# The lengths that a planner counts for two kinds of matmul, 512 and 288 columns, when it writes out the order of the work

## The chip, the cores and the metric

The kernel runs on one core of a Trainium2 chip. The metric is the device time of one execution in microseconds (us). Engines are named as in the profile: PE is TensorE, PEld its weight loads, DVE is VectorE, ACT is ScalarE, POOL is GpSimd, and SP is SyncE, which here only issues DMAs.

## The reference

The input x has 2048 rows of 576. It is normalised per row, and two things are made of the result: a self-attention with 32 heads of 18 columns, and a bilinear gated feed-forward block of width 4608. Everything is float32.

```python
xn = _layernorm(x)
q, k, v = split(xn @ wqkv)                       # 32 heads, 18 columns each
s = softmax(q @ k.T * 18 ** -0.5) @ v            # per head, 2048 x 2048 scores
s = merged_heads(s) @ wo
g = silu(((xn @ w_gate) * (xn @ w_up)) @ w_down)
out = x + s * g
```

## The kernel before

A first stage normalises x, turns it to columns and makes q, k and v, split into a high and a low part so that products of float32r operands come close to float32. A last stage multiplies the attention's result by `wo` (L1229) and puts the output together. Between them lies the main stage, some nine tenths of the time, and the change concerns it alone.

In the main stage nearly all matmuls have 64 rows of contraction, so two of them run beside each other, one in the upper half of the array (rows 0 to 63) and one in the lower (64 to 127). Each half works through a list of its own:

- *gate and up* products (`gu_op`, L678): 27 matmuls of 512 columns into one PSUM bank. The upper half makes "up" tiles, the lower "gate" tiles. The work is cut into 72 units of 256 hidden columns by 512 rows of x (18 units for each of four chunks of rows), with two tiles in a unit.
- *down* products (`down_op`, L720): 48 matmuls of 288 columns for each unit in each half, in four groups of 12, each group into a bank that DVE then adds to `acc` (`down_end`, L748). Six of the 12 read `hs`, the hidden rows of the half itself; the next six read `hx`, a copy of the other half's rows that DMAs bring (`turn_round`, L710). The last unit's copy is called `hxl`, and its weights `wdl`.
- *scores for the maxima* (`a_item`, L596): one matmul of 512 columns, then a maximum on DVE (L598). There are 2048 of them, one a head, row tile and column block.
- *scores for the exponentials* (`b_item`, L628): the same in the other orientation, then an exponential on ACT (L630), also 2048.

Between stretches of such work stand *visits* (`pv_group`, L639): up to seven row tiles of the exponentials are multiplied by v over the whole height of the array, 28 matmuls at a time, and DVE or ACT adds the result to `oc`. After a head's last visit `finish` (L651 to L656) turns and divides it on DVE and DMAs store it (L659).

The order of all this is written out when the program is built. `order()` keeps a planned clock for each half (`clk`), planned times at which engines and banks come free (`free`, `banks`), and planned landings of DMAs (`moved`). In a loop it takes the half whose clock is behind and gives it either a score, if the goal clock (`a_goal`, `b_goal`) says that one is due and its bank is free, or the next matmul of its list, which `stream()` yields. Each step moves that half's clock on by its length: LONG for a matmul of 512 columns (`a_next`, `b_next` and the gate and up products), SHORT for one of 288. All other durations are absolute numbers: 0.60 us for a maximum on DVE, 0.495 us for an exponential on ACT, 0.859 us for four matmuls of a visit, 0.24 MB per us for a DMA. `span`, and with it `pace`, the distance at which scores are due, is worked out from LONG and SHORT as well. The clock has no part in the execution: there the engines follow their queues and semaphores. Both halves are fed from the one PE queue, in its order.

Of the kernel before, what the change touches and what calls it, by code (L numbers as in the profile page):

```python
# [40 lines left out]
def kernel(  # L41
# [536 lines left out]
    with ExitStack() as mid:  # L578
# [264 lines left out]
            xi[t] = fin["ep"].tile([128, D], FT, name="xi", bufs=8)  # L843
            nc.sync.dma_start(xi[t], x2[rows, :])

        LONG, SHORT = 0.2335, 0.1335

        def stream(r):

# [449 lines left out]
```

## Time and profile before

| | |
|---|---|
| median of 3 runs | 2575.25 us (2573.8 to 2578.24) |
| the profiled execution's own time | 2576.35 us |
| its span on the core | 2574.6 us |
| PE busy | 2558.4 us, 99% of the span |
| DVE, ACT, POOL busy | 74%, 57%, 23% |
| main stage on PE | from 194.78 to 2510.43 us |
| granted TensorE clock | full speed in all slices |

Times within the run count from the start of the span. A matmul's own duration in the trace (389 ns for 512 columns) is longer than the distance at which matmuls of one half follow each other, since they are pipelined, and the two halves overlap. What a matmul costs is therefore read from the starts of matmuls of one half that follow each other without a wait.

### The profile page before, as it was taken

What the parts mean: (1) busy time and instruction counts of PE and PEld (TensorE: products, weight loads), DVE (VectorE), ACT (ScalarE), POOL (GpSimd) and SP (SyncE); (2) the same over time, 40 slices, a digit from 0 to 9 for tenths busy, and PEclk for the clock granted to TensorE, in tenths of its full rate; (3) what the DMA queues carried; (4) which work ended last, traced back from release to release, by engine and by line L of the source; (5) the groups of instructions that cost most, each with busy time, mean ns of one, the idle gap of its engine ahead of it and who ended that gap; (6) DMA issues with size and microseconds to landing.
All of it is one profiled execution on the core that took longest, in us unless ns stands there. A gap on an engine that the chain in (4) does not pass through costs nothing.

```text
span 2574.6 us, 59106 instructions
## 1 busy us (share of the span) xinstructions
PE 2558.4 (99%) x24360; PEld 2080.9 (81%) x24360; DVE 1917.3 (74%) x3377; ACT 1458.4 (57%) x2688; POOL 594.3 (23%) x663
## 2 busy tenths in 40 slices
PE   8999999999999999999999999999999999999999
PEld 7899887778878778877877788877787888887779
DVE  6209777778778888877788888877788888777527
ACT  5222666666655555655555565655555665555561
POOL 3214434434421111111111112111111211111125
PEclk9999999999999999999999999999999999999999
DMA  7799988887785666665686656656686666665567
GB/s 245 234 281 275 273 228 232 225 222 218 220 202 180 179 181 178 171 183 153 179 196 177 172 161 191 178 157 177 169 198 156 177 187 174 174 178 166 155 182 254
DMA packets 195897, 504.57 MB, mean 196 GB/s; under 512 B 58112, under 2 KB 116352, under 8 KB 156588
## 3 DMA queue, kind: packets, MB, share of 16 engines
q1 hardware_dynamic: 185676, 489.05, 67.9%
q0 software_dynamic: 9952, 11.74, 1.7%
q8 instruction: 192, 3.15, 0.6%
q14 instruction: 77, 0.63, 0.1%
HBM read 312.21 MB, written 107.61 MB: 163 GB/s over the span
## 4 chain that ended last, share of the span: by engine, by line
PE 98%; DVE 1%; DMA 1%; ACT 0%; issue 0%; SPq 0%
PE pg L678 35%; PE pg L639 17%; PE pg L720 16%; PE pa L596 11%; PE pb L628 9%; PE pg L402 2%; PE pa L348 2%; PE pb L348 2%; PE pg L1229 1%; PE pa L1229 1%; PE pb L1229 1%; DMA xc<-sx 0%; DMA xin<-in_A_x_dram 0%; PE pg L334 0%; DVE mx L598 0%; DVE xcx L338 0%
## 5 line engine op out<-in xcount | busy, mean ns | idle before, releaser
L598 DVE TENSOR_REDUCE mx<-pa 128x1 f32<-128x512 f32 x2048 | 1361.8, 685 | 150.2 <-PE pa L596 67.4
L630 ACT ACTIVATE pt<-pb 128x512 f32<-128x512 f32 x2048 | 1155.0, 598 | 549.0 <-PE pb L628 464.7
L678 PE MATMUL pg<-xc,wgu 64*128 64x512 f32 x7776 | 1381.0, 389 | 1.5 <-DMA xc<-sx 1.5
L678 PEld LDWEIGHTS pg<-xc,wgu 64*128 64x128 f32 x7776 | 1032.3, 184 | 54.7 <-DMA xc<-sx 3.1
L628 PE MATMUL pb<-pair,ring 64*128 64x512 f32 x2006 | 783.8, 397 | 0.5 <-ACT us L683 0.5
L596 PE MATMUL pa<-pair,ring 64*128 64x512 f32 x2001 | 781.1, 396 | 0.4 <-DVE mx L598 0.4
L720 PE MATMUL pg<-wd,hs 64*128 64x288 f32 x3408 | 531.3, 292 | 1.2 <-DVE acc L748 1.2
L720 PE MATMUL pg<-wd,hx 64*128 64x288 f32 x3408 | 524.6, 292 | 0.0
L720 PEld LDWEIGHTS pg<-wd,hs 64*128 64x128 f32 x3408 | 468.3, 185 | 6.6 <-DVE acc L748 1.9
L720 PEld LDWEIGHTS pg<-wd,hx 64*128 64x128 f32 x3408 | 462.7, 185 | 3.6 <-DMA hx<-hs 0.5
L639 PE MATMUL pg<-pt,vt 128*32 128x512 f32 x4096 | 454.8, 594 | 0.0
L694 POOL TENSOR_TENSOR hs<-us,hs 128x512 fp32r<-128x512 f32 x144 | 186.1, 1292 | 1120.3 <-ACT hs L693 1101.8
L596 PEld LDWEIGHTS pa<-pair,ring 64*128 64x128 f32 x2001 | 362.6, 184 | 92.0 <-issue 47.8
L628 PEld LDWEIGHTS pb<-pair,ring 64*128 64x128 f32 x2006 | 364.0, 184 | 11.3 <-ACT pt L630 1.4
L639 PEld LDWEIGHTS pg<-pt,vt 128*32 128x32 f32 x4096 | 125.5, 110 | 283.8 <-issue 280.7
L645 DVE TENSOR_TENSOR oc<-oc,pg 128x512 f32<-128x512 f32 x69 | 47.5, 688 | 319.2 <-PE pg L639 319.0
L748 DVE TENSOR_TENSOR acc<-acc,pg 128x288 f32<-128x288 f32 x544 | 234.6, 445 | 26.7 <-PE pg L720 24.0
L693 ACT ACTIVATE hs<-us 128x512 fp32r<-128x512 f32 x144 | 91.0, 632 | 155.8 <-DVE us L690 151.7
L659 POOL DMA_DIRECT2D sot<-oc x124 | 64.0, 523 | 327.7 <-DVE oc L656 325.4
L618 POOL DMA_DIRECT2D pair<-mt x128 | 78.0, 615 | 225.2 <-DVE mt L613 218.6
L643 ACT ACTIVATE oc<-pg 128x512 f32<-128x512 f32 x32 | 19.2, 599 | 189.3 <-PE pg L639 189.3
L194 POOL TENSOR_TENSOR wgu<-wraw,wgu 128x384 fp32r<-128x384 f32 x108 | 108.4, 1017 | 68.2 <-ACT wgu L193 47.8
(141 smaller groups left out, 1381.9 us busy)
## 6 DMA issues: line engine op xcount, KB each, us to landing
wgu<-swg SPq DMA_DIRECT2D x102, 1152.0 KB
hx<-hs SPq DMA_DIRECT2D x142, 512.0 KB
wd<-swd SPq DMA_DIRECT2D x50, 1152.0 KB
swg<-wgu SPq DMA_DIRECT2D x36, 1152.0 KB
pair<-sqk SPq DMA_DIRECT2D x192, 144.0 KB
ring<-sqk SPq DMA_DIRECT2D x384, 72.0 KB
swd<-wd SPq DMA_DIRECT2D x18, 1152.0 KB
sqk<-hl SPq DMA_DIRECT2D x32, 512.0 KB
```

The source lines that it names most:

```text
L194: nc.gpsimd.tensor_tensor(w[:, 9 + b:12 + b, :], raw[:, b:b + 3, :], w[:, b:b + 3, :].bitcast(FT), op=OP.subtract)
L348: nc.tensor.matmul(p, wq[b, a], xcs[c][:, e, :], start=n == 0, stop=n == len(PAIRS) - 1)
L596: nc.tensor.matmul(p, q[rows, t * 128:(t + 1) * 128], k[rows, c * 512:(c + 1) * 512], start=True, stop=True)
L598: nc.vector.tensor_reduce(mx[h][:, t, c:c + 1], p, axis=AX.X, op=OP.max)
L628: nc.tensor.matmul(p, k[rows, t * 128:(t + 1) * 128], q[rows, c * 512:(c + 1) * 512], start=True, stop=True)
L630: nc.scalar.activation(pt[t, c], p, AF.Exp, scale=scale)
L639: nc.tensor.matmul(p[32 * c:32 * c + 32, :], vt[h // 2][:, t, 6 * (h % 2):6 * (h % 2) + 32], pt[t, c], start=t == ts[0], stop=t == ts[-1])
L678: nc.tensor.matmul(ps, gw[n][half[r], a, :], xg[i][half[r], e, :], start=k == 0, stop=k == len(TERMS) - 1)
L693: nc.scalar.activation(hj[:, 0, :], h32, AF.Copy)
L694: nc.gpsimd.tensor_tensor(hj[:, 1, :], h32, hj[:, 0, :].bitcast(FT), op=OP.subtract)
L720: nc.tensor.matmul(ps[:, 0:HALF], (hx if k else hs)[u][half[r], j, a, s * 128:(s + 1) * 128], dw[u][half[r], k, j, e, :], start=n == 0, st ...
L748: nc.vector.tensor_tensor(a, a, ps[:, 0:HALF], op=OP.add)
```

## The change

One line gives the planner other lengths for its two kinds of matmul. No instruction is added or taken away: both programs have the same 7776, 6912, 2048, 2048 and 2048 matmuls at L678, L720, L596, L628 and L639, and 74 visits of the same sizes. What changes is the order in which they stand, nearly everywhere in the main stage.

```diff
-        LONG, SHORT = 0.2335, 0.1335
+        LONG, SHORT = 0.2285, 0.1325
```

PE's queue from the last visit on. `wd` is the down weights of the last unit but one, `wdl` those of the last unit. Before:

```order
L628 MATMUL pb<-pair_1153,ring 128x512
L639 MATMUL pg<-pt,vt 32x512 x16
L720 MATMUL pg<-wdl,hs 128x288 x12
L720 MATMUL pg<-wdl,hxl 128x288 x12
L720 MATMUL pg<-wdl,hs 128x288 x12
L720 MATMUL pg<-wdl,hxl 128x288 x12
L720 MATMUL pg<-wdl,hs 128x288 x11
```

Now, with 51 rows of the `wd` products of both halves left out behind the last one shown:

```order
L678 MATMUL pg<-xc,wgu 128x512 x9
L639 MATMUL pg<-pt,vt 32x512 x16
L678 MATMUL pg<-xc,wgu 128x512 x2
L720 MATMUL pg<-wd,hs 128x288
L678 MATMUL pg<-xc,wgu 128x512
L720 MATMUL pg<-wd,hs 128x288
L678 MATMUL pg<-xc,wgu 128x512
L720 MATMUL pg<-wd,hs 128x288 x2
L678 MATMUL pg<-xc,wgu 128x512
L720 MATMUL pg<-wd,hs 128x288 x2
```

Before, only the last unit's down products (48 in each half) stand behind the last visit. Now there are the down products of two units (96 in each half), and ahead of them the last matmuls of the last gate tile: one of the upper half, six of the lower.

The end of these down products, now, where one unit passes to the next:

```order
L720 MATMUL pg<-wd,hs 128x288
L720 MATMUL pg<-wd,hx 128x288
L720 MATMUL pg<-wd,hs 128x288 x4
L720 MATMUL pg<-wd,hx 128x288 x6
L720 MATMUL pg<-wdl,hs 128x288 x12
L720 MATMUL pg<-wdl,hxl 128x288 x12
L720 MATMUL pg<-wdl,hs 128x288 x12
```

The ten matmuls in two rows of four and six are of the lower half alone, which ends the unit later than the upper one; after them both halves begin the last unit together.

DVE's queue at the same place. Here `oc`, `tp` and `rc` belong to `finish` of the last head, `us` to the gate tile (gate times up, L690), `acc` to the down products. Before:

```order
L645 TENSOR_TENSOR oc<-oc,pg 128x512
L651 STREAM_TRANSPOSE tp<-oc 128x512
L654 RECIPROCAL rc<-tp 128x16
L655 TENSOR_TENSOR tp<-tp,rc 128x16x18
L656 STREAM_TRANSPOSE oc<-tp 128x512
L748 TENSOR_TENSOR acc_11514<-acc_11514,pg 128x288 x4
```

Now:

```order
L645 TENSOR_TENSOR oc<-oc,pg 128x512
L651 STREAM_TRANSPOSE tp<-oc 128x512
L654 RECIPROCAL rc<-tp 128x16
L655 TENSOR_TENSOR tp<-tp,rc 128x16x18
L656 STREAM_TRANSPOSE oc<-tp 128x512
L690 TENSOR_TENSOR us<-pg,us 128x512
L748 TENSOR_TENSOR acc_11500<-acc_11500,pg 128x288 x4
```

The last gate tile's multiplication has moved behind `finish` of the last head; before, it stood ahead of the last visit.

SP's queue at the same place: `hxl` is the other half's rows for the last unit, `wor` the weights of the last stage, `o0` to `o2` attention results for it, `sot` the last head's store. Before:

```order
L710 DMA hxl_37573<-hs_37567 64x1024
L710 DMA hxl_37573<-hs_37567 64x1024
L796 DMA wor_37697<-in_A_wo_dram 128x576
L796 DMA wor_37697<-in_A_wo_dram 128x576
L796 DMA wor_37697<-in_A_wo_dram 128x576
L796 DMA wor_37697<-in_A_wo_dram 128x576
L798 DMA wor_37697<-in_A_wo_dram 64x576
L798 DMA wor_37697<-in_A_wo_dram 64x576
L814 DMA o0_37864<-sot_81 128x512
L814 DMA o1_37865<-sot_81 128x512
L814 DMA o2_37866<-sot_81 128x512
```

Now:

```order
L814 DMA o0_37720<-sot_81 128x512
L814 DMA o1_37721<-sot_81 128x512
L710 DMA hxl_37668<-hs_37662 64x1024
L710 DMA hxl_37668<-hs_37662 64x1024
L796 DMA wor_37784<-in_A_wo_dram 128x576
L796 DMA wor_37784<-in_A_wo_dram 128x576
L796 DMA wor_37784<-in_A_wo_dram 128x576
L796 DMA wor_37784<-in_A_wo_dram 128x576
L798 DMA wor_37784<-in_A_wo_dram 64x576
L798 DMA wor_37784<-in_A_wo_dram 64x576
L814 DMA o2_37722<-sot_81 128x512
```

Two loads of attention results have moved ahead of the last `hxl` pair, the third one has moved behind the six loads of `wor`.

## Rows read from the trace of the kernel before

**Rows 1.** The page: busy time, and the chain that ended last.

```profile
PE 2558.4 (99%) x24360; PEld 2080.9 (81%) x24360; DVE 1917.3 (74%) x3377; ACT 1458.4 (57%) x2688; POOL 594.3 (23%) x663
...
PE 98%; DVE 1%; DMA 1%; ACT 0%; issue 0%; SPq 0%
```

**Rows 2.** Waits: engine, line, releaser: us in total, times, longest.

```profile
PE pg L678 <- DMA xc<-sx: 1.5, 3, 1.0
PE pg L720 <- DVE acc L748: 1.2, 2, 0.8
...
PEld pg L678 <- DMA xc<-sx: 3.1, 4, 1.4
```

**Rows 3.** Timeline: start us, us, engine, line. PE, both halves in 512 columns.

```profile
2480.31 0.39 PE L628 MATMUL pb<-ring,pair 64*128 64x512 f32 x1
2480.31 1.75 PE L678 MATMUL pg<-xc,wgu 64*128 64x512 f32 x13
2481.90 0.40 PE L628 MATMUL pb<-ring,pair 64*128 64x512 f32 x1
```

**Rows 4.** Timeline, PE, from the last visit to the last stage.

```profile
2499.56 3.64 PE L639 MATMUL pg<-pt,vt 128*32 128x512 f32 x32
2503.13 1.06 PE L720 MATMUL pg<-wdl,hs 64*128 64x288 f32 x12
...
2505.64 0.95 PE L720 MATMUL pg<-wdl,hxl 64*128 64x288 f32 x12
2506.70 1.42 PE L720 MATMUL pg<-wdl,hs 64*128 64x288 f32 x12
2507.83 1.08 PE L720 MATMUL pg<-wdl,hxl 64*128 64x288 f32 x12
...
2509.42 1.08 PE L720 MATMUL pg<-wdl,hxl 64*128 64x288 f32 x12
2510.43 1.86 PE L1229 MATMUL pa<-wos,hi 128*128 128x288 f32 x12
```

**Rows 5.** Timeline, PE, the main stage's start.

```profile
194.78 0.49 PE L678 MATMUL pg<-xc,wgu 64*128 64x512 f32 x1
...
195.12 0.39 PE L678 MATMUL pg<-xc,wgu 64*128 64x512 f32 x1
```

**Rows 6.** The chain in order of time: one visit of 28.

```profile
295.60 6.14 PE pg L639 x56
```

**Rows 7.** Timeline, DVE, the same place: `finish`, then sums.

```profile
2503.34 0.69 DVE L645 TENSOR_TENSOR oc<-oc,pg 128x512 f32<-128x512 f32 x1 [3.65 <-PE pg L639]
...
2505.59 0.71 DVE L656 STREAM_TRANSPOSE oc<-tp 128x512 f32<-128x512 f32 x1
2506.23 1.51 DVE L748 TENSOR_TENSOR acc<-acc,pg 128x288 f32<-128x288 f32 x4
```

**Rows 8.** Timeline, DVE, ACT, POOL, SP: last gate tile to `hxl`.

```profile
2490.89 0.69 DVE L690 TENSOR_TENSOR us<-pg,us 128x512 f32<-128x512 f32 x1
...
2491.62 0.63 ACT L693 ACTIVATE hs<-us 128x512 fp32r<-128x512 f32 x1
...
2492.33 1.29 POOL L694 TENSOR_TENSOR hs<-us,hs 128x512 fp32r<-128x512 f32 x1 [9.70 <-ACT hs L693]
...
2493.65 1.10 SPq L710 DMA_DIRECT2D hxl<-hs  x2
2494.85 2.58 SPq L796 DMA_DIRECT2D wor<-in_A_wo_dram  x4
```

**Rows 9.** DMA issues: KB each, median us from issue to landing.

```profile
sot<-oc POOLq DMA_DIRECT2D x124, 36.0 KB, 2.8
...
out_dram<-ys POOLq DMA_DIRECT2D x10, 288.0 KB, 5.6
```

**Rows 10.** Timeline, ACT and POOL: splitting the weights of the last stage.

```profile
2500.16 0.68 ACT L834 ACTIVATE wos<-wor 128x576 fp32r<-128x576 f32 x1
...
2500.91 1.42 POOL L835 TENSOR_TENSOR wos<-wor,wos 128x576 fp32r<-128x576 f32 x1 [7.29 <-ACT wos L834]
```

**Rows 11.** Timeline, PE, at the first change of rows of x.

```profile
749.43 0.50 PE L678 MATMUL pg<-xc,wgu 64*128 64x512 f32 x2 [0.98 <-DMA xc<-sx]
```

**Rows 12.** Timeline, PE, a long list beside a short one: first and last.

```profile
738.62 0.39 PE L678 MATMUL pg<-xc,wgu 64*128 64x512 f32 x1
...
739.99 0.39 PE L678 MATMUL pg<-xc,wgu 64*128 64x512 f32 x1
```

## The prediction

> **What bounds the kernel now.** I read the page first. PE is busy 99% of the span, and 98% of the chain that ended last is PE's [rows 1]. So only PE's queue counts. Next come the waits of PE: the longest sums that name another engine or a DMA are 1.5 and 1.2 us [rows 2]. A reader who stops there would say that nothing is left to win. But a matmul stays "busy" in these views while its half runs late, so I read distances between starts instead. In a stretch where both halves run matmuls of 512 columns, seven of the lengths stand between two score matmuls of one half: 2481.90 - 2480.31 = 1.59 us, or 0.227 each [rows 3]. Where both halves run 288 columns, 24 matmuls, 12 in each half, take 2509.42 - 2507.83 = 1.59 us, or 0.1325 each [rows 4]. These are undisturbed lengths.
>
> With them the main stage can be added up from the order. It lasts from 194.78 to 2510.43, or 2315.7 us [rows 4, 5]. Its 74 visits are 72 of 6.14 [rows 6] and two of 3.64 us [rows 4], together 449.4. In each of the 75 stretches between them I counted each half's matmuls, at 0.227 and 0.1325, and took the longer half: 1808.9 us together. The remainder, 57 us, is what restarts behind visits, last matmuls ahead of them, and waits cost, 0.76 us a stretch. A new order can change only this remainder and the balance of the halves.
>
> **What the change does.** It gives the planner lengths nearer to 0.227 and 0.1325 for the 512 and 288 columns; no duration on the chip depends on them. Every engine's and DMA's planned time stays, so the planner now counts some 2% more matmuls into the same wait. I went through the order for what that moves.
>
> *Visits.* 74 as before, of the same sizes, with the same total of matmuls: 0 us.
>
> *Balance.* The same count over the new order gives 1809.8 us, +0.9. Most of it is in the last stretches: in one the lower half has 3.3 us of work more than the upper, since the upper may not yet begin its down products, and behind the last visit it has 1.1 us more. The bounds are 0 (the other half uses the time for a later stretch, which the order hardly allows) and +1.8, if the longer halves' own distances are those of a disturbed stretch too.
>
> *The scores' spacing.* For each score I took the distance, in these lengths, from the score two before it, which used the same bank. Below 1.4 us lie 672 of the maxima before and 682 now, below 1.3 us 276 and 303 of the exponentials. DVE and ACT are asked about as often, and about as soon, as before: 0 us, with -3 to +3 as bounds, a twentieth of the remainder each way.
>
> *The end, where the sum can be followed.* Let V be the start of the last visit, 2499.56 before. Down products resume at V+3.57 [rows 4], and DVE is in `finish` from V+3.78 to 2505.59+0.71, which is V+6.74 [rows 7]. Before, the down products wait for DVE there: two steps of 12 matmuls take 2506.70-2505.64 = 1.06 and 2507.83-2506.70 = 1.13 us where 0.80 is undisturbed, and the last stage starts 0.2 late in the same way, 0.8 us in all.
>
> Now the last gate tile's six matmuls also stand behind V, and its multiplication (0.69) waits in DVE's queue behind `finish`: V+7.43. The casts on ACT (0.63) and POOL (1.29) follow, with the steps of 0.05 between them [rows 8], and SP issues the `hxl` pair from V+9.45; its second DMA, by half of the pair's 1.10, at V+10.0. The lower half's matmuls: restart at V+3.57, 0.11 for the restart (at the main stage's start the second matmul follows after 0.34 instead of 0.227 us [rows 5]), 6 x 0.227, 48 x 0.1325, so it would begin the last unit at V+11.4. But its second group of 12, due at V+6.6, needs one of four banks. The gate's own comes free at V+7.43 and the first down group's only when DVE has added it behind that, so I count 0.9 us of wait: V+12.3. It reads the rows of `hxl` that land last in its tenth matmul, 9 x 0.1325 later, at V+13.5.
>
> When do they land? No row has the landing of this DMA of 256 KB. The nearest are a store of 36 KB at 2.8 and one of 288 KB at 5.6 us [rows 9]. That makes V+12.8 to V+15.6, a wait of 0 to 2.1. I take the middle, 4.2, because the size is that of the longer row while the queue is SP's and not POOL's: V+14.2, a wait of 0.7. Both waits together are 1.6 where there were 0.8, so +0.8, between 0 and +2.2.
>
> *`wor` behind it.* SP starts these loads at V+10.55 now; before, they were issued ahead of the last visit (2494.85 [rows 8]). The last stage begins at V+12.3+48 x 0.1325+0.7 = V+19.4, and its sixth matmul needs the third low part: landing 4.2, a cast of 0.68 and three of 1.42 on POOL [rows 10], V+19.7, against V+20.0. That hides it by 0.3. At 5.6 for the landing it is 1.1 late. I take 0, with bounds 0 and +1.1.
>
> *Chunk boundaries.* At the first change of rows of x PE waits for them [rows 11]; its weight loads wait 3.1 us for `xc` in the whole run [rows 2], all of it there. The DMAs and their readers stand at the same distances in the new order, 12.6 us at the least, counted in lengths. So this wait stays: 0 us.
>
> **Sum.** +0.9 + 0.8 = +1.7 on the profiled execution's own 2576.35 us: 2578.0. The median of the runs shown is 1.1 lower, 2575.25, and the new one is compared with such runs, so I predict 2577.0. The bounds above add up to -3 and +8.1 around the profiled time.
>
> **Rivals.**
>
> *The truer ratio of lengths pays.* The old ratio takes 0.227 x 0.1335/0.2335 = 0.1298 for a short one where it lasts 0.1325. Where one half is in short and the other in long matmuls, the half with the short ones falls 0.0027 us behind the written order with each. In the order before, 2349 of the 6912 stand so. With the new ratio, 0.0009 remains, and 2349 x 0.0018 = 4.2 us can be saved if all of it had been passed on to the end. Against it: where a long list stands beside a short one, seven long ones in a row start 1.37/6 = 0.228 us apart [rows 12], hardly more than the 0.227 beside long ones, so the lag mostly fits into what the halves may run apart. With this and the same waits otherwise, 2577.0 - 4.2 = 2572.8; with a tenth of the remainder (5.7) gone as well, since the scores stand later against DVE, 2567.
>
> The Trainium skill, "TensorE: Matmul & The Clock Gate", Part 3 on row and column tiling, says that matmuls start and end strictly in program order, and only weight loads are pulled ahead. By that rule a half that lags holds up the other at once, and this rival would be paid in full; the trace's 0.228 beside 0.227 shows little of it here.
>
> *A load that arrives late.* The forecast has x at the later chunk boundaries, and the score operands, hidden as before. If the second boundary, whose loads stand 12.7 us ahead of their readers at the least, behaves as the first one does, at a like distance, 3.1 us are added: 2580.1, and 2583.2 if the third, at 14.1 us, does too. For it: one load of a head's keys has moved from 8.3 to 6.0 us ahead of its first reader, close to the longest landing in [rows 9]. Against it: before, the second boundary had loads 12.2 us ahead, and PE has no longer wait for them than those of the first. It decides from about 3.5 us of new waits on.
>
> *The change does nothing.* The order differs in most rows of PE's queue, so this is out; that it does nothing to the time is the forecast.
>
> **Chances.** The forecast, with rests between -5 and +5 us, 0.60. The truer ratio with fewer waits 0.18, the late load 0.22. A measurement here can tell a difference of about 0.2%, 5.2 us, from none: between 2570.1 and 2580.4 is "the same". The ratio alone (2572.8) would still be the same, and becomes faster with the fewer waits; I give 0.17 to that, 0.61 to the same and 0.22 to slower. The range, 2568 to 2584, reaches from the ratio with most of the fewer waits to both boundaries late. The forecast's own is 2573 to 2581.
>
> **What would show it.** Right: 74 visits and PE at 98% of the chain again; PE from the last visit to the last stage some 8.5 us longer than the 10.9 of before (V+19.4), with the lower half waiting for DVE about V+7 and for `hxl` about V+13.5; the stage ahead of it shorter by some 7 us, so that the last stage starts within 3 us of 2512. Wrong: `hxl` landed ahead of its reader (the landing was over-priced); waits for `xc`, `ring` or `pair` at places other than about 745 us (a late load); a remainder well below 57 us in the same count (the ratio pays).

## The result and the profile after

The changed kernel takes 2584.43 us (median of 7 runs, 2582.93 to 2584.98). The ratio to the kernel before is 1.0030, with a 95% interval from 1.0018 to 1.0042. It is slower by 0.3%, some 8 us; forecast were 2577.0 us and no difference. The profiled execution took 2584.43 us too, with a span of 2582.6 us.

The page of after, against [rows 1]: PE is as busy as before, but DVE and the DMAs now have 3% of the chain that ended last, where they had 2%, and PE's share is 96% instead of 98%.

```profile
PE 2559.4 (99%) x24360; PEld 2089.2 (81%) x24360; DVE 1923.5 (74%) x3377; ACT 1463.7 (57%) x2688; POOL 595.2 (23%) x663
...
PE 96%; DVE 2%; DMA 1%; SPq 0%; issue 0%; ACT 0%; POOL 0%; ACTq 0%
```

The waits of PE after, as in [rows 2] (us in total, times, longest). Three of them were not among the long ones before: the maxima on DVE, the `hx` rows, and, in the last line, one wait of 1.8 us in the last stage.

```profile
PE pg L720 <- DVE acc L748: 2.3, 4, 1.0
PE pa L596 <- DVE mx L598: 2.1, 4, 0.7
PE pg L720 <- DMA hx<-hs: 1.9, 2, 1.7
PE pa L1229 <- ACT hi L822: 1.8, 1, 1.8
```

Before, PE waited for the maxima once:

```profile
PE pa L596 <- DVE mx L598: 0.4, 1, 0.4
```

PE from the last visit on, the rows that answer to [rows 4] (start us, us, engine, line, [idle before <-releaser]):

```profile
2494.50 3.64 PE L639 MATMUL pg<-pt,vt 128*32 128x512 f32 x32
...
2501.88 0.40 PE L720 MATMUL pg<-wd,hs 64*128 64x288 f32 x1 [0.50 <-DVE us L690]
...
2508.34 0.67 PE L720 MATMUL pg<-wdl,hxl 64*128 64x288 f32 x6 [0.24 <-DMA hxl<-hs]
...
2513.72 0.53 PE L1229 MATMUL pa<-wos,hi 128*128 128x288 f32 x2
2516.01 2.22 PE L1229 MATMUL pa<-wos,hi 128*128 128x288 f32 x10 [1.76 <-ACT hi L822]
2518.03 2.69 PE L1229 MATMUL pb<-wos,hi 128*128 128x288 f32 x12
2520.56 3.35 PE L1229 MATMUL pg<-wos,hi 128*128 128x288 f32 x24
```

The last visit starts at V = 2494.50, the last stage at 2513.72. Here are the stage's inputs. First the chain in order of time, from the last gate tile's multiplication to the ten matmuls that waited in the last stage:

```profile
2501.17 0.66 DVE us L690
...
2502.57 1.31 POOL hs L694
...
2503.89 0.47 SPq L710
...
2505.05 0.60 SPq L796
...
2506.74 0.48 SPq L796
...
2509.06 6.24 DMA o<-sot
...
2515.32 0.64 ACT hi L822
...
2516.01 2.22 PE pa L1229 x10
```

SP's queue holds, in this order, the two last `hxl` transfers (L710), six loads of `wor` (L796, L798) and the third block of o. It stands still until POOL has the `hs` rows of the last gate tile; then all nine go out within some 5 us. The third block of o is issued ninth and lands after 6.24 us, and PE's third matmul waits for its cast. ACT's casts of the first and the third `wor` load show when these land, and the last row is the third low part on POOL, as in [rows 10]:

```profile
2509.00 0.69 ACT L834 ACTIVATE wos<-wor 128x576 fp32r<-128x576 f32 x1 [6.51 <-DMA wor<-in_A_wo_dram]
...
2512.98 0.69 ACT L834 ACTIVATE wos<-wor 128x576 fp32r<-128x576 f32 x1 [0.38 <-DMA wor<-in_A_wo_dram]
...
2513.74 1.41 POOL L835 TENSOR_TENSOR wos<-wor,wos 128x576 fp32r<-128x576 f32 x1 [0.15 <-DMA wor<-in_A_wo_dram]
```

The same place in windows (us; busy time of PE, PEld, DVE, ACT, POOL; granted TensorE clock as a share of full speed; share of the DMA engines; GB/s):

```profile
2500.00:2504.00 4.00, 3.50 (x52) 3.26 (x51) 3.12 (x8) 0.63 (x1) 1.30 (x1) 1.00 0.00 0
2504.00:2508.00 4.00, 4.00 (x54) 3.86 (x51) 1.95 (x5) 0.00 (x0) 0.00 (x0) 1.00 0.75 179
2508.00:2512.00 4.00, 3.75 (x55) 3.66 (x56) 1.64 (x4) 1.81 (x4) 1.43 (x1) 1.00 1.03 320
2512.00:2516.00 4.00, 2.25 (x30) 1.86 (x26) 2.99 (x6) 1.96 (x5) 2.84 (x2) 1.00 0.97 292
2516.00:2518.00 2.00, 1.99 (x10) 1.99 (x11) 0.90 (x2) 1.10 (x2) 1.39 (x1) 0.67 0.82 249
2518.00:2520.50 2.50, 2.50 (x13) 2.50 (x13) 0.00 (x0) 0.00 (x0) 1.54 (x2) 0.58 0.90 284
```

The DMA engines move nothing for 4 us, are at 0.75 in the next four, and full (1.03 and 0.97) for the 8 us after them. Behind the wait the granted clock falls to its lower level, 1.2 GHz, for some 3.4 us (full speed less 0.67 and 0.58, over 2.0 and 2.5 us): the ten matmuls from 2516.01 and the next twelve take 2.02 and 2.53 us, from group to group, where before, whose first group starts at 2510.43 [rows 4], has 1.70 for a first and 1.59 for a second twelve:

```profile
2512.13 1.76 PE L1229 MATMUL pb<-wos,hi 128*128 128x288 f32 x12
2513.72 3.35 PE L1229 MATMUL pg<-wos,hi 128*128 128x288 f32 x24
```

This is not peculiar to the one profiled execution. A fall of 3.4 us to half the clock takes 1.7 of 2584, or 0.0007, off an execution's mean granted clock. All seven executions of after have a mean of 0.999, while ten of the eleven of e8 (below), in which the wait is gone, have 1.000. In the kernel before, `wor` was issued 15.6 us ahead of the last stage [rows 4, 8] and the DMAs worked at 0.96 while the last visit began:

```profile
2496.00:2500.00 4.00, 4.00 (x36) 3.16 (x38) 1.36 (x3) 3.53 (x7) 0.00 (x0) 1.00 0.96 299
```

From the first to the last matmul of the last stage after takes 63.2 us, before 59.4; from there to the end 5.6 against 4.7. That is 4.7 of the 8.0 us between the two spans. The main stage, up to the last stage's start, is 4.2 longer (2319.9 against 2315.7), and it starts 0.9 earlier.

### The profile page after: what moved, and what is told of

Same layout as the page of the kernel before. It is cut to its first block, busy times and chain, and to the rows that moved or that the text cites. A ratio compares the mean times of both kernels' runs of the same rounds, so it can differ in the third digit from the quotient of the medians.

```text
span 2582.6 us, 59080 instructions
## 1 busy us (share of the span) xinstructions
PE 2559.4 (99%) x24360; PEld 2089.2 (81%) x24360; DVE 1923.5 (74%) x3377; ACT 1463.7 (57%) x2688; POOL 595.2 (23%) x663
## 4 chain that ended last, share of the span: by engine, by line
PE 96%; DVE 2%; DMA 1%; SPq 0%; issue 0%; ACT 0%; POOL 0%; ACTq 0%
PE pg L678 34%; PE pg L639 17%; PE pg L720 15%; PE pa L596 12%; PE pb L628 8%; PE pg L402 2%; PE pa L348 2%; PE pb L348 2%; PE pg L1229 1%; DMA xc<-sx 1%; PE pb L1229 1%; PE pa L1229 1%; DVE mx L598 1%; DMA hx<-hs 0%; DMA o<-sot 0%; DVE acc L748 0%
## 5 line engine op out<-in xcount | busy, mean ns | idle before, releaser
L678 PE MATMUL pg<-xc,wgu 64*128 64x512 f32 x7776 | 1381.6, 389 | 1.2 <-DMA xc<-sx 0.8
L678 PEld LDWEIGHTS pg<-xc,wgu 64*128 64x128 f32 x7776 | 1044.5, 184 | 54.6 <-DMA xc<-sx 2.3
L628 PE MATMUL pb<-pair,ring 64*128 64x512 f32 x2013 | 785.5, 396 | 0.6 <-ACT us L683 0.6
L596 PE MATMUL pa<-pair,ring 64*128 64x512 f32 x2001 | 779.0, 395 | 2.1 <-DVE mx L598 2.1
L720 PE MATMUL pg<-wd,hs 64*128 64x288 f32 x3408 | 536.4, 292 | 2.9 <-DVE acc L748 2.3
L720 PE MATMUL pg<-wd,hx 64*128 64x288 f32 x3408 | 522.2, 292 | 1.9 <-DMA hx<-hs 1.9
L720 PEld LDWEIGHTS pg<-wd,hs 64*128 64x128 f32 x3408 | 468.8, 185 | 9.3 <-DVE acc L748 3.6
L720 PEld LDWEIGHTS pg<-wd,hx 64*128 64x128 f32 x3408 | 459.2, 185 | 6.0 <-DMA hx<-hs 2.4
L639 PE MATMUL pg<-pt,vt 128*32 128x512 f32 x4096 | 454.8, 594 | 0.1
L596 PEld LDWEIGHTS pa<-pair,ring 64*128 64x128 f32 x2001 | 362.8, 184 | 88.9 <-issue 48.6
L628 PEld LDWEIGHTS pb<-pair,ring 64*128 64x128 f32 x2013 | 365.4, 184 | 8.7 <-issue 1.2
L639 PEld LDWEIGHTS pg<-pt,vt 128*32 128x32 f32 x4096 | 125.5, 110 | 283.5 <-issue 279.4
L643 ACT ACTIVATE oc<-pg 128x512 f32<-128x512 f32 x32 | 19.2, 599 | 183.2 <-PE pg L639 183.2
```

The source lines that it names most:

```text
L596: nc.tensor.matmul(p, q[rows, t * 128:(t + 1) * 128], k[rows, c * 512:(c + 1) * 512], start=True, stop=True)
L628: nc.tensor.matmul(p, k[rows, t * 128:(t + 1) * 128], q[rows, c * 512:(c + 1) * 512], start=True, stop=True)
L639: nc.tensor.matmul(p[32 * c:32 * c + 32, :], vt[h // 2][:, t, 6 * (h % 2):6 * (h % 2) + 32], pt[t, c], start=t == ts[0], stop=t == ts[-1])
L678: nc.tensor.matmul(ps, gw[n][half[r], a, :], xg[i][half[r], e, :], start=k == 0, stop=k == len(TERMS) - 1)
L720: nc.tensor.matmul(ps[:, 0:HALF], (hx if k else hs)[u][half[r], j, a, s * 128:(s + 1) * 128], dw[u][half[r], k, j, e, :], start=n == 0, st ...
```

## Experiments

For every run three numbers are worked out, the first two as in the prediction: the sum of the longer halves over the 75 stretches, at 0.227 and 0.1325 us; the remainder, which is the main stage less 449.4 us of visits and less the longer halves; and the last stage from its first to its last matmul. Old lengths are 0.2335 and 0.1335, new ones 0.2285 and 0.1325.

| run | lengths | longer halves | remainder | last stage | median, us | ratio to before, 95% |
|---|---|---|---|---|---|---|
| before | old | 1808.9 | 57.3 | 59.4 | 2575.25 | 1 |
| after | new | 1809.8 | 60.7 | 63.2 | 2584.43 | 1.0030 [1.0018, 1.0042] |
| e1_o2_first | new | 1809.8 | 60.4 | 64.5 | 2584.18 | 1.0032 [1.0020, 1.0045] |
| e5_wor_early | new | 1809.8 | 59.5 | 60.9 | 2581.19 | 1.0018 [1.0009, 1.0027] |
| e8_all_wor_early | new | 1809.8 | 59.0 | 59.4 | 2578.17 | 1.0011 [1.0002, 1.0020] |
| e6_old_wor_late | old | 1808.9 | 58.4 | 62.6 | 2579.38 | 1.0012 [1.0003, 1.0021] |
| e2_pace | new | 1812.3 | 58.3 | 61.9 | 2582.86 | 1.0026 [1.0016, 1.0036] |
| e3_long_only | 0.2285, 0.1335 | 1813.2 | 57.4 | 61.0 | 2585.44 | 1.0039 [1.0024, 1.0054] |
| e4_short_only | 0.2335, 0.1325 | 1812.0 | 64.2 | 60.2 | 2587.35 | 1.0045 [1.0032, 1.0059] |
| f1_old_early | old | 1810.2 | 61.6 | 59.4 | 2580.57 | 1.0017 [1.0008, 1.0026] |
| f2_old_sooner | old | 1807.8 | 58.1 | 59.4 | 2576.41 | 1.0002 [0.9993, 1.0011] |
| f3_old_skew | old | 1812.3 | 58.6 | 61.4 | 2583.63 | 1.0037 [1.0023, 1.0050] |
| f4_new_first | new | 1811.3 | 60.1 | 59.4 | 2579.21 | 1.0013 [1.0005, 1.0022] |
| e7_new_early_cured | new | 1809.3 | 59.6 | 63.6 | 2582.49 | 1.0028 [1.0018, 1.0038] |

(The three columns come from one profiled execution, the ratio from all. In the batches of the later runs the kernel before had medians of 2575.4 to 2576.4, so the ratios are to be compared, not the medians. A profiled execution is not always a typical one: that of e3 is 2.9 us below its median, that of e6 2.3 above.)

**e1_o2_first: the third block of o ahead of `wor`.** First I took only the place of the block that PE had waited for.

```diff
                                 if r and n == 2 * len(units) - 1:
+                                    while loads and loads[0][:2] == (fetch_o, (2, 0)):
+                                        loads.pop(0)
+                                        fetch_o(2, 0)
                                     wo_load()
```

> The changed kernel, with one load moved in SP's queue: o2, the third block of attention results for the last stage, goes ahead of the six loads of wor instead of behind them. PE's order is that of the changed kernel to the last row. Theory A (the last stage starves: PE stood 2.0 us before the last stage's third matmul for the cast of o2, and then ran 3.4 us at half the granted clock): both go, the wait (2.0) and what the clock cost (1.7), so about 2580.7 us against 2584.4, no wait of PE at L1229 and a granted clock of 1.0 throughout the last stage's first ten us. Theory B (the loss lies in the order of the main stage): within 1 us of 2584.4.

It gained nothing. Two waits stand where one was, the second for `wor`'s low part on POOL:

```profile
2513.26 0.67 PE L1232 MATMUL pa<-wos,hi 128*128 128x288 f32 x2
2514.68 0.67 PE L1232 MATMUL pa<-wos,hi 128*128 128x288 f32 x3 [0.74 <-ACT hi L822]
2516.32 2.05 PE L1232 MATMUL pa<-wos,hi 128*128 128x288 f32 x7 [0.98 <-POOL wos L835]
```

The first is `wor`'s too: ACT casts three `wor` loads ahead of the third block of o, and the second of these had made it wait until 2512.28. By its number this is theory B's result. But the wait has only changed its name, so it is not the one block's place. I read it as the whole group of loads going out too late, which e5 and e8 test below.

**e2_pace, e3_long_only, e4_short_only: other orders, and each half of the change alone.** PACE is 1.008 instead of 1.005 in the first, whose last gate tile ends ahead of the last visit again, so that its `wor` loads go out 13.1 us ahead of the last stage, at the start of that visit; the others have one of the two new lengths each.

```diff
-        PACE, SKEW, PULL, FIRST, ROWS = 1.005, 3.0, 3.0, 2.0, 6.0
+        PACE, SKEW, PULL, FIRST, ROWS = 1.008, 3.0, 3.0, 2.0, 6.0     # e2
-        LONG, SHORT = 0.2285, 0.1325
+        LONG, SHORT = 0.2285, 0.1335     # e3
+        LONG, SHORT = 0.2335, 0.1325     # e4
```

> The changed kernel with the planner's PACE at 1.008 instead of 1.005, so that scores are due later and attention ends later: behind the last visit stand 9.0 us of matmuls instead of 13.9, and the last gate matmul, and with it the loads of wor, is back ahead of the last visit. The sum of the longer halves is 1812.3 us against 1808.9 before and 1809.8 changed. Theory A (end of the stage: starved last stage, plus balance of the halves): 2575.25 + 3.4 = 2578.7, with no wait of PE at L1229. Theory B (512-column length 0.2285 makes the main stage's waits longer, whatever the end): 2583 or more.

> Only the length for 512 columns is changed (0.2285, with 0.1335 for 288). Sum of the longer halves 1813.2, that is +4.3 on before; behind the last visit 17.6 us of matmuls; o2 stands ahead of the hxl pair in SP's queue, but wor is issued only 12.7 us ahead of the last stage, as in the changed kernel. Theory A: 2575.25 + 4.3 + 0 to 1 for a late wor = 2579.5 to 2580.5, without a clock of 0.5 at the last stage's start. Theory B (the length for 512 columns is what costs): 2584 or more.

> Only the length for 288 columns is changed (0.1325, with 0.2335 for 512). Sum of the longer halves 1812.0, +3.1 on before; the last gate matmul stands 16.2 us ahead of the last stage, so wor and the loads behind it have time. Theory A: 2578.4, no wait at L1229. Theory B (the length for 512 columns costs): 2575 to 2577, like before. The rival of the prediction, that a truer ratio pays, has here a ratio of 1.762, further from the measured 1.713 than before (1.749): slower by some us if it holds.

All three missed what theory A asked for. e3 came out where theory B had it, but e4, which theory B had at 2575 to 2577, is the slowest of all, so the length for 512 columns is not the cause by itself either. e2 starts its last stage without a wait (later in it PE waits 2.2 us for the first products on DVE) and has its longer halves 2.5 us higher than after, which together leave it about where after is, 0.26% over before. The two halves of the change do not add up to the whole (0.39% and 0.45% each, 0.30% together): not the lengths' values, but the particular order that comes of them, seemed to set the time. So the next four runs draw the order anew with other constants, three of them with the old lengths.

**f1 to f4: other draws.**

```diff
-        EARLY = 0.17
+        EARLY = 0.171                                        # f1, old lengths
-        QUICK, LAST, SOONER = 0.75, 0.75, 10.0
+        QUICK, LAST, SOONER = 0.75, 0.75, 9.8                # f2, old lengths
-        PACE, SKEW, PULL, FIRST, ROWS = 1.005, 3.0, 3.0, 2.0, 6.0
+        PACE, SKEW, PULL, FIRST, ROWS = 1.005, 3.05, 3.0, 2.0, 6.0   # f3, old lengths
+        PACE, SKEW, PULL, FIRST, ROWS = 1.005, 3.0, 3.0, 2.1, 6.0    # f4, new lengths
```

> The lengths of before stay (0.2335, 0.1335); another constant of the model (EARLY, 0.170 to 0.171) only draws the order anew. The last gate tile ends ahead of the last visit as in before, the longer halves sum to 1810.2 us (before: 1808.9). Theory L, the false lengths themselves give an order that flows better: 2575 to 2576.5. Theory C, each drawn order has its own cost (longer halves, plus the tail if wor starts after the last visit): +1.3, so 2576.6. Theory P, the order of before is a picked one and any other draw loses: 2581 or more.

> The lengths of before stay; SOONER 10.0 to 9.8 draws the order anew. Last gate tile ahead of the last visit, longer halves sum to 1807.8 us (before: 1808.9). Theory L: 2575 to 2576.5. Theory C: -1.1, so 2574.2. Theory P: 2581 or more.

> The lengths of before stay; SKEW 3.00 to 3.05 draws the order anew. Here the last gate tile ends after the last visit, with three loads of o ahead of wor as in after, and the longer halves sum to 1812.3 us (before: 1808.9). Theory L: 2575 to 2576.5. Theory C: +3.4 for the halves and +3.7 for the starved last stage, so 2582.4. Theory P: 2581 or more (it does not tell this run from C).

> The lengths of after (0.2285, 0.1325) with FIRST 2.0 to 2.1, which draws an order whose last gate tile ends ahead of the last visit, as in before; longer halves sum to 1811.3 us. Theory L, the true lengths are what loses: 2582 or more. Theory C: +2.4 over before, so 2577.7. Theory P: 2581 or more.

Theory L, that the old lengths as such are better, falls: f3 has them and loses 0.37%, f4 has the new ones and loses 0.13%. Theory P, that no other draw comes near, falls by f2, which cannot be told from before. Theory C is nearest: f3 was expected at 2582.4 and measured 2583.63, f4 at 2577.7 and 2579.21. In part this is luck: f3's last stage takes 2.0 us more than before's and not 3.7, and its profile has a wait of 2.36 us for the first `hx` that the theory doesn't know. It missed f1 and f2 by some 4 and 2 us. In f1's profile a part of that is seen: a load of a head's keys is late at the first change of rows of x, and the clock is at its lower level behind it (timeline of PE, then windows):

```profile
759.31 0.47 PE L628 MATMUL pb<-pair,ring 64*128 64x512 f32 x1 [2.21 <-DMA ring<-sqk]
```

```profile
756.00:760.00 4.00, 1.79 (x16) 0.95 (x16) 1.38 (x2) 1.38 (x3) 0.00 (x0) 1.00 0.90 214
760.00:764.00 4.00, 4.00 (x24) 1.00 (x20) 0.00 (x0) 0.41 (x1) 0.00 (x0) 0.57 0.23 94
```

f4 has the same wait, 2.21 us, and the same drop. In before PE waits there for ACT, 0.5 us, with the clock at 1.00. Not every execution has the drop: six of f4's eleven have a mean granted clock of 1.000 and take 2575.98 to 2579.96 us, the other five 0.999 and 2579.21 to 2583.08. Seven of f1's eleven have 1.000 too and still take 2578.80 to 2580.97, so the drop is not the whole of what f1 loses.

**e5, e6, e8: the loads alone, TensorE's order unchanged.** These three have the matmul order of after (e5, e8) or of before (e6), matmul for matmul; only SP's queue differs. In e5 and e8 `gate_end` calls `wo_load` ahead of the last `turn_round`, with the third block of o in front:

```diff
+            if n == 2 * len(units) - 1:
+                wo_load(range(2))        # e5: two of the loads; e8: range(5), all
             if u == 0 and j or u == len(units) - 1:
                 turn_round(u, j)
...
-                                    wo_load()
+                                    wo_load(range(2, 5))   # e5: the others
```

In e6 the kernel before gets the late load of after:

```diff
-                                    wo_load()
...
                     f(*a)
+                    if a == (2, 1):
+                        wo_load()
```

> After, with TensorE's order unchanged matmul for matmul; only SP's queue differs at the last gate tile: the third block of o and the first two of the six wor loads stand ahead of the last hxl transfers, the other four wor loads behind them as before. Theory A (in after, 2.0 us of waiting at the start of the last stage and 1.7 us of half clock behind it come from wor and o2 landing late): the wait falls under 0.5 us, the granted clock stays 1.0 there, last stage from its first to its last matmul 59.4 to 60 us instead of 63.2, and 2580.5 to 2581.5. Rival B (the loads share the same 16 DMA engines, so hxl is late instead and the loss moves into the last down tiles): 2583.5 or more.

> Before, with TensorE's order unchanged matmul for matmul; only SP's queue differs: the six wor loads stand behind the six loads of o (they issue at about 7 us ahead of the last stage instead of 15.6). Theory A: the last stage starves as in after, a wait of 1.5 to 2.5 us and a drop of the granted clock behind it, last stage 62 to 64 us instead of 59.4, so 2578 to 2580. Rival B (the loads have slack, and what after loses lies elsewhere): 2575.5, no wait and clock 1.0.

> After, with TensorE's order unchanged matmul for matmul; SP issues the third block of o and all six wor loads ahead of the last hxl transfers (e5_wor_early had two of the six there), in the 7 us in which SP only waits for the last gate tile. Theory A (what is left of the tail's loss in e5, 1.5 us of the last stage from the product's late inputs and 0.9 us behind the last matmul, is the same loads landing late): last stage 59.4 to 60 us and 4.7 us behind it, as in before, so 2578.5 to 2579.5; what is left over before, some 3 us, is the longer halves (+0.9), the two waits around the last gate tile (+0.8) and the first stretch. Rival B (e5 has taken all that the loads cost): 2580.5 to 2582. Rival C (the bigger block ahead of hxl makes hxl late): 2583 or more, with a wait on hxl over 1 us.

All three came out about where theory A had the time: 2581.19, 2579.38 and 2578.17 us, the last 0.3 below its range. In e5 the wait at the start of the last stage is gone, but that stage takes 60.9 us and not 59.4 to 60, with a wait of 1.3 us on DVE later in it; in e8 this is gone too. SP's queue and PE in e8:

```profile
2492.16 2.01 SPq L821 DMA_DIRECT2D o<-sot  x3
2494.22 1.84 SPq L803 DMA_DIRECT2D wor<-in_A_wo_dram  x4
2496.11 2.23 SPq L805 DMA_DIRECT2D wor<-in_A_wo_dram  x2
2502.12 1.12 SPq L712 DMA_DIRECT2D hxl<-hs  x2
```

```profile
2511.96 1.86 PE L1236 MATMUL pa<-wos,hi 128*128 128x288 f32 x12
2513.66 1.76 PE L1236 MATMUL pb<-wos,hi 128*128 128x288 f32 x12
2515.26 3.35 PE L1236 MATMUL pg<-wos,hi 128*128 128x288 f32 x24
```

The six `wor` loads go out between 2494.2 and 2498.3, in the 8 us up to 2502.1 in which SP otherwise only waits for the last gate tile. The last stage then runs without a wait at full clock and takes 59.4 us as before. In e6 the kernel before is made to starve (PE, the start of its last stage):

```profile
2512.59 0.40 PE L1230 MATMUL pa<-wos,hi 128*128 128x288 f32 x1 [0.54 <-ACT hi L822]
2513.69 0.66 PE L1230 MATMUL pa<-wos,hi 128*128 128x288 f32 x3 [0.69 <-ACT hi L822]
2515.55 1.20 PE L1230 MATMUL pa<-wos,hi 128*128 128x288 f32 x7 [1.20 <-POOL wos L835]
```

Here the expectation missed in one thing: the waits came, in three pieces, but in this profile the clock did not fall (it is 1.00 there). Five of e6's eleven executions have a mean granted clock of 0.999 or 0.998; where it fell in them, no trace shows.

**e7_new_early_cured: the loads of e5 in another draw with the new lengths** (EARLY 0.171).

> The lengths of after (0.2285, 0.1325), EARLY 0.171 instead of 0.170 (another draw of the order, longer halves 1809.3 us against 1808.9 of before and 1809.8 of after), and the SP order of e5_wor_early. Theory C (an order costs its longer halves, its tail and its waits, whatever the lengths are called): +0.4 for the halves, 0 for the tail, +1 to +2.5 for the first stretch as in the other draws, so 2576.5 to 2578.5. Theory P (the order of before is a picked one and no draw comes near it): 2580 or more.

It missed: 2582.49 us, where theory P had it, though f2 has already shown a draw that comes near. The start of its last stage is free of waits, but the blocks of o that stand behind the other four `wor` loads land late, their low parts on DVE too, and DVE comes late to the products that free the first banks. Behind that wait the clock falls (0.55 from 2531.0 to 2534.5):

```profile
2530.26 1.03 PE L1236 MATMUL pa<-wos,hi 128*128 128x288 f32 x6 [2.08 <-DVE ys L1245]
```

Its last stage takes 63.6 us for that. e8 was run after it with all the loads early; this draw with all of them early was not run. No version tried is faster than before; f2 comes nearest.

## Where the prediction was right and where it was wrong

The forecast was no difference: 2577.0 us, with 2573 to 2581 as its own. It is slower by 0.3%, clear of the noise. The wider range, up to 2584, about reaches the result (2583.0 by the ratio, 2584.43 by the median). That is luck: its upper end was there for late loads of x at two chunk boundaries, and these did not come: PE waits 0.8 us for `xc` in after, 1.5 before.

**The step that failed is "`wor` behind it".** I took 0 for it, with 1.1 us as the upper bound. e8 against after shows what late loads cost: the ratio goes from 1.0030 to 1.0011, 4.9 us, give or take some 4, with no matmul moved; in the profiles the last stage shrinks by 3.8 and what follows it by 1.6. e6 shows the same from the other side: before with its `wor` loads late loses 0.12%. The step had the mechanism and the times of issue: `wor` was put at V+10.55, and SP issues it at 2505.05, V+10.55 to the digit. It went wrong in three ways.

- *The landing.* I took 4.2 us, the middle of two rows of stores, of 36 and 288 KB [rows 9], and one time of issue for all the loads. The first `wor` load lands in time for its cast at 2509.00, 3.95 us after the issue, but the third is issued 1.7 us after the first, at 2506.74, and lands some 6.2 later, at 2512.98; the block of o behind them takes 6.24. The DMA engines are full from 2508 on. In this profile it alone would have cost some 0.7: the third low part is ready at 2515.15, V+20.65, where my sum had V+19.7 and its matmul was due at about 2514.4. That lies within my bound of 1.1.
- *What else stands in SP's queue.* The third block of o, behind `wor`, was not in the sum at all, though the order of the queue was before me. It set the end of the wait: 2516.01 where the third matmul would have been at about 2514.0. e1 shows that putting it first only hands the wait to `wor`, which then lands later still.
- *The clock.* The wait of 2.0 us was followed by 3.4 us at 1.2 GHz, and this cost (2.02 + 2.53) - (1.42 + 1.59), or 1.5 us, with 1.42 for ten of the twelve in 1.70. No term of mine had it.

**V to the last stage: right.** Forecast V+19.4; measured 2513.72 - 2494.50 = 19.2. The gate's multiplication ends at V+7.3 (forecast 7.43) and the `hxl` pair is issued at 2503.89, V+9.4 (9.45). The wait for DVE is 0.5 (0.9 forecast), that for `hxl` 0.24 (0.7): the landing of 4.2 was about right for this one (its second DMA, issued at 2504.41, landed within 3.9), ahead of which the DMA engines had moved nothing for 4 us. The stage ahead of V is shorter by 4.1 us measured from the main stage's start (2300.7 against 2304.8), where I said some 7: the other 3 are lost ahead of V, and the next paragraphs tell how.

**The sum without the loads: right within what can be measured.** I had +0.9 for the balance and +0.8 for the waits, +1.7 us. e8, after without the late loads, measures 0.11% over before, 2.8 us, between 0.5 and 5.2. What it is made of was not as forecast, as the scores' spacing shows.

**Balance: right as a cost, its price not shown.** In f3, e2, e3 and e4 the longer halves are 3 to 4 us above before's and all four lose 0.26 to 0.45%. The sum of the three columns of the table can't show what a longer half costs, since the remainder is what is left of the measured main stage. The remainder can: if a longer half cost nothing, it would be smaller by as much. In e2, e3 and f3 it is 57.4 to 58.6, no smaller than before's 57.3. But it holds PE's waits too, and these are longer than before's; without them (worked out below) f3's remainder is 52.1 against 53.6, with the same lengths and longer halves 3.4 above. By this one pair some 2 of the 3.4 us arrive at the end. The same count gives 52.8 for e6, which has before's order, so it is good to about 1 us. The profile is no exact account of the median either: the three columns together stand 6.0 us over before's in e3, which measures 0.39%, or 10. What I did not ask is where before's sum lies among the orders that the planner can draw: of 34 others with the old lengths that I wrote out and counted (three are f1 to f3, the rest was not run), 30 have longer halves above 1808.9, up to 1813.2. With that I would have put the forecast for any redrawn order higher.

**The scores' spacing: not 0, but within its bounds.** PE's waits for the maxima are 2.0 to 2.1 us in all four profiles with after's order (after, e1, e5, e8) and 0.4 in both with before's (before, e6). The down products wait 2.3 us for the sums on DVE in the same four and 1.2 in the same two. So these 2.7 us come with the order, and the counts of spacings did not show them.

**The truer ratio pays: not in the time, though perhaps in a part of it.** Its mark was a remainder well below 57. It lies between 57.3 and 64.2 in all fourteen rows of the table. The Trainium skill's rule named in the prediction ("TensorE: Matmul & The Clock Gate", Part 3), that matmuls start and end in program order, would make a lagging half hold up the other and the true ratio save time; no run here shows this in the time. e3 speaks against it: its ratio, 1.712, is the nearest to the measured 1.713, and it loses 0.39%. e4, with 1.762 the furthest, is the slowest, as the rival asked, but by far more than 4.2 us.

But the remainder also holds PE's waits for others (those over 0.15 us): 3.7 us in the main stage before, 8.7 in after, 7.4 in e8. Without them it is 53.6 in before, 52.0 in after and 51.5 in e8. Over all runs it is 49.2 with the truest ratio (e3), 50.0 to 52.0 with the new lengths, 52.1 to 54.1 with the old, and 53.7 in e4. So some 1.5 of the rival's 4.2 us may have been paid (51.5 to 52.0 in the four profiles with after's order, 52.8 and 53.6 in the two with before's), and the added waits took them back. The draws differ in more than the ratio, so this is not shown.

**A load that arrives late: right as a danger, at another place.** after loses to loads, but to those of the last stage and not at the chunk boundaries; f1 and f4 do lose 2.2 us and a slow clock to a late load of keys at the first boundary. e1 and e8, which have after's matmul order, wait 1.4 and 1.1 us for keys there, where after itself waits 0.6 for ACT: whether this load is late differs between executions of one order.

**What stays open.** In the first stretch, PE waits for the first `hx` for 1.66 us in after and for less than can be seen in before. This is not the order: e6, which has before's order, waits 2.21 us there, and e5 and e8, which have after's, 1.04 and 0.57.

```profile
274.23 0.40 PE L720 MATMUL pg<-wd,hx 64*128 64x288 f32 x1 [1.66 <-DMA hx<-hs]
```

```profile
275.39 0.40 PE L720 MATMUL pg<-wd,hx 64*128 64x288 f32 x1 [2.21 <-DMA hx<-hs]
```

A difference of two single profiles holds up to 2 us of this kind, so the 2.8 us between e8 and before cannot be assigned one by one. e4's remainder of 64.2 is nearly all waits of PE: they come to 10.6 us in its main stage against 3.7 before, 4.0 of them for the maxima, and without them it is 53.7, as before's. Why its order makes PE wait so often stays open.

## What to carry to other kernels

When a planner writes out the order, any edit to its constants draws a new order, and the one that stands may be among the best of many draws (f2 alone of the thirteen other versions could not be told from before); add up the longer halves of some neighbouring draws before forecasting "no change". Look for the place where a queue that issues loads in order stands still for a late producer: put loads that need nothing from it ahead of the wait, as e8 does; in that one draw the last stage then took as long as before's. Price a load by what is in flight with it, not by the latency of one alone.

## What the runs showed of the hardware

A PE wait of about 2 us was followed by some 3.4 us at 1.2 GHz in four profiles: after (2.0 us in the last stage), f1 and f4 (2.21 us for keys) and e7 (2.08 us); in e1 the fall came with two shorter ones (0.74 and 0.98). It did not come behind every such wait. e6 has 2.21 us and f3 2.36 us for `hx` at 275 us, and the granted clock stays 1.00 in the windows around them (e6):

```profile
272.00:276.00 4.00, 1.79 (x21) 1.46 (x19) 1.32 (x2) 1.51 (x3) 0.00 (x0) 1.00 0.99 304
276.00:280.00 4.00, 4.00 (x56) 3.84 (x54) 3.54 (x8) 2.82 (x6) 1.43 (x2) 1.00 0.77 288
```

e2 has the very wait of e7, on DVE's first product in the last stage, for 2.21 us, and no fall behind it:

```profile
2531.58 1.03 PE L1229 MATMUL pa<-wos,hi 128*128 128x288 f32 x6 [2.21 <-DVE ys L1238]
```

```profile
2532.00:2536.00 4.00, 4.00 (x32) 4.00 (x31) 4.00 (x8) 2.14 (x4) 3.38 (x6) 1.00 0.92 254
```

e6's three waits at the start of its last stage, 2.4 us together, brought none either. So the length of the wait does not tell these apart; what does was not tested. In after, loads of 256 and 288 KB on SP's queue landed within 4 us when they went out second and third of nine, and after 6.2 us when they went out fifth and ninth, with the DMA engines' share going from 0.00 over 0.75 to 1.03.
